# A four-layer attention and feed-forward kernel: one gate input loaded as a row and spread by a product, and a new operation order

## The chip, the cores and the metric

The kernel runs on one core of a Trainium2 chip. The number that counts is the device time of one launch in microseconds (us): 546.09 us before the change, the median of three runs (545.96 to 546.21).

A core has five instruction streams that run side by side, each strictly in its own written order: TensorE (PE, matrix products; its weight loads are listed apart as PEld), VectorE (DVE), ScalarE (ACT), GpSimd (POOL) and SyncE (SP, which here only issues DMAs). They wait for each other through semaphores. Products land in PSUM, eight banks of 128 x 512 words; everything else sits in SBUF, 128 partitions wide.

## What is computed

The input x has 2048 rows of 512. Four steps follow each other, each of the form x = x + f(layernorm(x)): attention, feed-forward, attention, feed-forward, with the same weights both times.

- Attention has 32 heads of width 16 and works in four segments of 512 rows. In a segment, scores = q kT / 4 under a causal mask, softmax, times v. Beside it runs a linear memory of the earlier segments: with phi(t) = t + 1 for t > 0 and exp(t) otherwise, a_mem = phi(q) M / (phi(q) z), where M and z gather phi(k)T v and phi(k) over the earlier segments. The head's output is g a_mem + (1 - g) a_dot, then the product with wo.
- g = sigmoid(beta), and **beta** is one vector of 32 numbers, one for each head. The kernel needs exp(beta) and exp(-beta) as 128 x 32 tiles, the same in every partition.
- Feed-forward: gelu(x w_gate) * (x w_up), then w_down, with an inner width of 1792.

## The kernel before

**Stages.** Eight passes k = 0 to 7: four segments of the first attention and feed-forward, four of the second. Within a pass come the layernorm of 4 tiles of 128 rows, their transposes, the q, k and v products, 72 score pieces in rounds, the products of probabilities with v ("flushes", line 954), wo, gate, up and down. Passes overlap: the feed-forward of pass k supplies PE with work while ACT does the exps of later scores.

**Who sets the order.** Nothing is scheduled by a compiler. The function `order` walks a clock model while it emits: it keeps a clock for each engine (`Clocks`, `Engine`), posts every operation with a ready time and a slack, and picks the next by those. `POLICY` holds some fifty numbers that steer the choice: due times of products (`qk_due`, `up_due`), slacks (`exp_slack`, `kb_slack`), how much later POOL may take over a DVE operation (`xn_pool`, `cut_pool`), how many score rounds may be ahead (`early`, `starve`). `CHANGES` can replace some of them in windows of 20 model microseconds (`Policy.move`); before the change it is empty. Once emitted, the order of each engine is fixed.

**How products are issued.** `product` (line 464) writes a 128-wide product in one of two forms. At line 476 it is one weight load and one matmul over the whole array ("whole"); at line 471 it is four weight loads and four matmuls on strips of 32 columns ("columns"), used where PE is already in that form for a flush. Scores (line 938) use a third form, strips of 16 or 32 rows ("rows"). When a bank is free but no item is ready, PE does a filler product on the tile `warm`, which is thrown away.

**The start.** This part is written by hand, not by the model:

1. SP and ACT each issue two of the four first tiles of x (line 314); ACT then issues the load of `beta_bc` to all 128 partitions (line 315); SP goes on with four halves of wk and wq, x of segment 1, wv, x of segment 2 (line 305).
2. PE does 15 products on `warm` (line 349) to be busy while the input arrives.
3. DVE takes the statistics of three tiles (line 1183), ACT of the fourth (lines 1198 and 1199). Straight after, ACT takes the two exps of beta (lines 1202 and 1203).
4. DVE writes the normalized tiles (line 544), PE transposes them (line 596), ACT copies tiles 0 and 1 out and DVE tiles 2 and 3 (lines 599 and 601), and PE does the first k and q products (lines 909 and 914), which ACT and DVE copy out (lines 1228 to 1237). DVE finishes the gate constants (lines 389 and 391), and the first scores begin.

From there on the model runs. It is told what the start took by constants: PE's clock 10.6, ACT 11.1, DVE 11.0, the DMA queue free at 13.0, x of segments 1 and 2 not before 11.85 and 14.8, v products not before 13.4.

**Other lines that come up.** 396: DVE writes the gate's column beside v. 417 and 422: masked copies of k on DVE, POOL or ACT. 461 and 462: copies out of PSUM on DVE or ACT. 514 and 522: layernorm statistics. 586: later transposes on PE. 745 and 764: phi. 1027: the addition to x. 1068, 1054 and 1151: gelu, 1151 over several tiles at once (`gelu_tiles`). 1396: the exps of the scores.

Of the kernel before, what the change touches and what calls it, by code (L numbers as in the profile page):

```python
# [11 lines left out]
ACT = mybir.ActivationFunctionType  # L12
# [3 lines left out]
BF16 = mybir.dt.bfloat16  # L16
I32 = mybir.dt.int32

P = 128
D = 512  # L20
H = 32
# [26 lines left out]
def round_of(t):  # L48
# [9 lines left out]
BANKS = 8  # L58
# [3 lines left out]
URGENT, SOON, NORMAL = -4.0, -1.5, 0.0  # L62
# [4 lines left out]


POLICY = dict(
    flush_wait=31.348, piece_slack=5.108, kb_slack=25.115, mem_slack=-15.103, margin=2.314, qk_due=0.572,  # L70
    e_q=-1.218, e_k=1.714, exp_slack=-25.107, e_slack=9.023, phi_slack=17.383, gelu_slack=6.274,
    act_evict=8.464, first_evict=0.965, gate_step=0.061, up_due=-0.553, up_step=0.062, down_due=2.078,
    down_step=0.526, upd_due=0.786, kb_act=6.552, vz_slack=-10.454, x_dve=-0.565, v0_due=-1.4, x1_at=-45.234,
    x2_at=18.289, x3_at=24.819, x3_load=-3.83, direct=4, gelu_tiles=4, look=1.769, lag=0.5, wv_at=8.591,
    xn_pool=7.037, kb_pool=5.303, cut_pool=1.107, at_pool=10.661, pe_turns=2, gate_due=0.765, shun=0.534,
    col_gap=3.33, hold=8, early=4.123, starve=0.308, near=-1.576, cap=4, soon=9.685, columns=0)

CHANGES = {
}
WINDOW = 20.0  # L80

# [204 lines left out]
def order(pol, nc, cst, seg, wrk, psp, A_x, A_wq, A_wk, A_wv, A_wo, A_beta, B_x, B_w_gate, B_w_up, B_w_down, out):  # L286

    ck = Clocks()
    ev = ck.ev
# [9 lines left out]
    wu_sb = cst.tile([P, KT, FF], BF16, name="wu_sb")  # L299
    wd_sb = cst.tile([P, FT, D], BF16, name="wd_sb")  # L300
    gel_sb = cst.tile([P, FT, L], BF16, name="gel_sb")
    beta_bc = cst.tile([P, H], BF16, name="beta_bc")

    def load(dst, src):
        nc.sync.dma_start(out=dst, in_=src)
# [6 lines left out]

    for j in range(TPS):
        (nc.scalar if j % 2 else nc.sync).dma_start(out=x_sb[:, j, :], in_=xv[:, j, :])
    nc.scalar.dma_start(out=beta_bc[:], in_=A_beta.partition_broadcast(P))
    for cols in (slice(0, D // 2), slice(D // 2, D)):
        load(w_att["k"][:, :, cols], w_view(A_wk)[:, :, cols])
        load(w_att["q"][:, :, cols], w_view(A_wq)[:, :, cols])
# [19 lines left out]
    warm = cst.tile([P, P], BF16, name="warm")  # L338
# [5 lines left out]
    ps_all = psp.tile([P, BANKS, L], F32, tag="ps", bufs=1, name="ps")  # L344
    pt_all = wrk.tile([P, PT_SLOTS, 4, UNIT], BF16, tag="pt", bufs=1, name="pt")

    def keep_warm(n, bank):
        for _ in range(n):
            nc.tensor.matmul(ps_all[:, bank, :], lhsT=warm[:], rhs=wide, start=True, stop=True)

    keep_warm(WARM, 0)

    mhalf = cst.tile([P, TPS, 1], F32, name="mhalf")
    nc.gpsimd.memset(mhalf[:], -0.5)
# [21 lines left out]
    tmp_e2 = cst.tile([P, H], F32, name="tmp_e2")  # L376
    cden = cst.tile([P, H], BF16, name="cden")
    macc = cst.tile([P, 4, P], F32, name="macc")
    tmp_e = macc[:, 0, 0:H]
# [4 lines left out]
    def by_head(va):  # L384
        return va[:, 0:TPS * VW].rearrange("p (t a h e) -> p t h a e", t=TPS, a=2, e=DH + 1)
# [8 lines left out]
    def later_constants():  # L394
        def column(va):
            nc.vector.tensor_copy(out=va[:, 0:TPS * VW].rearrange("p (t g e) -> p t g e", t=TPS, e=DH + 1)[:, :, :, DH],
                                  in_=cden[:].unsqueeze(1).to_broadcast([P, TPS, H]))
            nc.vector.memset(va[:, TPS * VW:], 0.0)

        for n, va in enumerate(vaugs[-1:] + vaugs[:-1]):  # L400
            ck.dve.post(10.5 + pol.col_gap * n, URGENT if n < 1 else NORMAL,
                        (Port(0.5), lambda va=va: column(va), lambda t, n=n: ev.update({("column", n): t})))

    def on_dve_or_pool(ready, slack, later, fast, slow, emit, told):
# [35 lines left out]
    banks = [0.0] * BANKS  # L440
# [11 lines left out]
    def evict(ps, dst, src, told, slack=NORMAL):  # L452

        taken = []

        def end(t):
            ps.read(t)
            told(t)

        first = pol.first_evict if ("scores", 0) not in ev else pol.act_evict  # L460
        ck.dve.post(ck.made(), slack, (0.673, lambda: nc.vector.tensor_copy(out=dst(), in_=src()), end), taken=taken)
        ck.act.post(ck.made(), slack + first, (0.602, lambda: nc.scalar.activation(
            out=dst(), in_=src(), func=ACT.Copy), end), taken=taken)
# [25 lines left out]
    def dense(ps, pairs):  # L489
        n = len(pairs)  # L490
        return [(Clocks.MM[512], lambda i=i, l=l, r=r: product(ps()[:], l(), r(), i == 0, i == n - 1))
                for i, (l, r) in enumerate(pairs)]
# [117 lines left out]
    class Att:  # L610
# [14 lines left out]
        def add_items(self):  # L625
            k, s = self.k, self.s
# [53 lines left out]
            def v(j):  # L680
                ps = Psum()
                pairs = [(lambda kt=kt: self.norm.xnT[:, kt, j * P:(j + 1) * P], lambda kt=kt: w_att["v"][:, kt, :])
                         for kt in range(KT)]

                def done():
                    self.counted()
                    evict(ps, lambda: by_head(self.vaug)[:, j, :, :, 0:DH],
                          lambda: ps()[:].rearrange("p (h a e) -> p h a e", a=2, e=DH), v_there)

                def v_there(t):  # L690
                    ev["v", k, j] = t
                    self.n_v += 1
                    if self.n_v == TPS:
                        ck.at(t, lambda: ck.when(lambda: not k or ("flush", k - 1, KT - 1, 1) in ev, halves))

                def halves():
                    def half(va, rows, a):
                        return va[rows, 0:TPS * VW].rearrange("p (t a v) -> p t a v", t=TPS, a=2)[:, :, a, :]

                    for a in range(2):  # L700
                        ck.sp.post(ck.pe, pol.vz_slack, (0.62, lambda a=a: nc.sync.dma_start(
                            out=half(vz, slice(C * a, C * a + C), a), in_=half(self.vaug, slice(0, C), a)), vz_sent))

                def vz_sent(t):
                    self.n_vz += 1
                    t2 = max(t + 1.4 + pol.margin, ck.dma + 1.2)
                    if self.n_vz == 2:
                        ck.at(t2 - 0.2, lambda: ev.update({("vz", k): t2}))

                return Item(lambda: k - pol.qk_due + 0.04 + 0.01 * j if k else pol.v0_due,  # L710
                            lambda: ck.has(("xnTa", k, j)) and (k or ck.pe > max(pol.wv_at, 13.4)) and
                            ck.has(("column", min(k, SETS)), by=ck.pe + 0.9) and (k <= SETS or ("flush", k - SETS, 3, 1) in ev),
                            dense(ps, pairs), done, kind="v", ps=ps, after=("xnTa", k, j))

# [3 lines left out]
            for j in range(TPS):  # L718
                items.append(v(j))
# [479 lines left out]
    nc.scalar.activation(out=spare[:, 1, :], in_=x_sb[:, TPS - 1, :], func=ACT.Square, scale=root, bias=shift[:],  # L1199
                         accum_out=n0.mv[:, TPS - 1, 1:2])  # L1200

    nc.scalar.activation(out=tmp_e, in_=beta_bc[:], func=ACT.Exp)
    nc.scalar.activation(out=tmp_e2[:], in_=beta_bc[:], func=ACT.Exp, scale=-1.0)

    first_stats(0)
    first_stats(1)
# [12 lines left out]
    a0 = att[0]  # L1219
    a0.made()  # L1220
    half = L // 2
    n0.first_turn(0)
    n0.first_turn(1)
    n0.first_turn(2)
    n0.first_turn(3)
    ps1 = ps_all[:, 1, :]
# [11 lines left out]
    gate_constants()  # L1238
    ev["xnTa", 0] = 0.0
    ev.update({("xnTa", 0, j): 0.0 for j in range(TPS)})  # L1240
    ck.pe, ck.act.free, ck.dve.free, ck.pool.free, ck.sp.free = 10.6, 11.1, 11.0, 8.1, 7.6
    banks[0:4] = [10.8, 9.45, 9.9, 10.4]
    ev["q", 0, 0] = 10.35
    a0.n_qkv = 2
    a0.k_done(0, None, 11.2)
    later_constants()
    ck.dma = 13.0
    def last_input(t):
        ck.dma_load(t, 512)
        norm_of_input(3, max(pol.x3_at, ck.dma + 1.4), 1.0)  # L1250
# [11 lines left out]
    def norm_of_input(s, at, gap):  # L1262
        for j in range(TPS):
            ck.at(at + gap * j, lambda j=j: att[s].norm.stats(j, ck.pe))

    norm_of_input(1, max(pol.x1_at, 11.85), 0.5)
    norm_of_input(2, max(pol.x2_at, 14.8), 1.0)


    streams = [(k, t) for k in range(NK) for t in range(STEPS)]  # L1270
# [42 lines left out]
    def rounds_now(idle=False):  # L1313

        if not streams or phase[0] is not None and phase[1] > pol.hold or not rounds_ready(2):
            return 0
        n, left = len(free_pairs()), len(streams)
        wait = backlog()
        if n >= 2 and (idle or left <= 4 or wait < (pol.early if streams[0][0] < 1 else pol.starve)):
            return 2  # L1320
        return 0
# [101 lines left out]
    while streams or items or opened or ck.busy():  # L1423
# [5 lines left out]
        n = rounds_now()  # L1429
# [24 lines left out]
        n = rounds_now(True)  # L1454
# [18 lines left out]
def kernel(  # L1473
# [18 lines left out]
    ctx.enter_context(tc.manual_schedule(engines=MANUAL))  # L1492
    order(Policy(POLICY, CHANGES), tc.nc, cst, seg, wrk, psp, A_x, A_wq, A_wk, A_wv, A_wo, A_beta, B_x, B_w_gate, B_w_up, B_w_down, out)

# [30 lines left out]
```

## Time and profile before

| what | value |
|---|---|
| median of three runs | 546.09 us (545.96 to 546.21) |
| device time of the profiled execution | 545.75 us |
| its span, first to last instruction | 544.0 us, so 1.75 us lie around it |
| TensorE clock granted | 0.999 of full speed over the span |
| busy | PE 531.3, PEld 276.3, DVE 443.7, ACT 434.7, POOL 305.5 us |
| chain of work that ended last | PE 88%, DVE 7%, DMA 2%, issue 2% |
| DMA | 26.95 MB, a mean of 50 GB/s |

How to read it. The busy line says how long an engine had an instruction in flight; as matmuls overlap in the pipeline, a PE that is 98% busy is one that hardly ever stood idle, and says nothing of how fast it went. The chain of waits follows the end back to the start: at each step it names what released the instruction, or the instruction before it on the same engine. In the timeline, equal neighbours are merged, and what stands in brackets is the idle time before an instruction and what ended it. The list of waits sums such idle times by who waited for whom. A few per cent of the matmul records can be missing from a trace (here 61 of 9334), and where one is, the timeline shows an apparent gap of one product that is none.

### The profile page before, as it was taken

How to read it: one execution, taken by the hardware profiler on the slowest of the kernel's cores; microseconds unless marked ns; L12 is line 12 of the kernel's file. 1: busy time of each engine (PE TensorE's matmuls, PEld its weight loads, DVE VectorE, ACT ScalarE, POOL GpSimd, SP SyncE). 2: the span in 40 equal slices, each digit the busy share in tenths (PEclk: the TensorE clock that was granted, in tenths of full speed). 3: DMA queues.
4: the chain of work that ended last, by engine and by line, in shares of the span. 5: the costliest groups of instructions: out<-in, count | busy, mean ns of one | idle time of the engine just before them, and what ended most of it. 6: DMA issues, size and time to landing. Idle time of an engine off the chain costs nothing.

```text
span 544.0 us, 21276 instructions
## 1 busy us (share of the span) xinstructions
PE 531.3 (98%) x9273; PEld 276.3 (51%) x9334; DVE 443.7 (82%) x816; ACT 434.7 (80%) x540; POOL 305.5 (56%) x359
## 2 busy tenths in 40 slices
PE   8999999999999999999999999999999999999997
PEld 4454555454545444554545555545465456555444
DVE  6998999799988999779987998889586797786342
ACT  5999989988898989989899798996879977920330
POOL 4898786369746788339993468716753265300000
PEclk9999999999999999999999999999999999999999
DMA  8406511610331123310312250221320114100001
GB/s 249 117 13 192 118 20 13 176 33 22 45 56 21 26 40 58 44 40 7 41 32 49 33 72 3 41 32 23 78 52 3 22 21 82 24 3 22 19 0 40
DMA packets 64926, 26.95 MB, mean 50 GB/s; under 512 B 49216, under 2 KB 64832, under 8 KB 64832
## 3 DMA queue, kind: packets, MB, share of 16 engines
q1 hardware_dynamic: 64400, 25.31, 22.6%
q8 instruction: 73, 1.20, 0.9%
q10 hardware_dynamic: 432, 0.27, 0.2%
q14 instruction: 21, 0.17, 0.1%
HBM read 9.71 MB, written 2.10 MB: 22 GB/s over the span
## 4 chain that ended last, share of the span: by engine, by line
PE 88%; DVE 7%; DMA 2%; issue 2%; ACT 0%; ACTq 0%; SPq 0%; DVEq 0%
PE ps L476 46%; PE ps L471 26%; PE ps L938 8%; PE ps L954 7%; DVE st L514 1%; DVE x_sb L1027 1%; DMA beta_bc<-in_A_beta_dram 1%; DVE byq L971 1%; PE ps L586 1%; DVE phiq L745 1%; PE ps L584 1%; DMA phik<-e 0%; DMA amT<-am 0%; DVE xn L544 0%; DVE e L764 0%
## 5 line engine op out<-in xcount | busy, mean ns | idle before, releaser
L1396 ACT ACTIVATE pt<-ps 128x1024 bf16<-128x1024 f32 x288 | 278.9, 1025 | 44.6 <-PE ps L938 41.1
L1343 POOL TENSOR_SCALAR_AFFINE_SELECT pt<-pt 128x256 bf16<-128x256 bf16 (+1 forms) x192 | 107.0, 571 | 118.0 <-ACT pt L1396 112.0
L1092 DVE TENSOR_TENSOR gel_sb<-gel_sb,ps 128x512 bf16<-128x512 bf16 x112 | 75.3, 682 | 33.9 <-PE ps L476 25.0
L476 PE MATMUL ps<-xnT,wu_sb 128*128 128x512 bf16 x287 | 66.8, 379 | 1.4 <-issue 1.1
L476 PE MATMUL ps<-xnT,wg_sb 128*128 128x512 bf16 x261 | 62.6, 379 | 0.9 <-issue 0.5
L764 POOL TENSOR_SCALAR e<-e 128x512 bf16<-128x512 bf16 x37 | 57.9, 1565 | 1.8 <-ACT e L741 0.7
L971 DVE STREAM_TRANSPOSE byq<-ps 128x512 f32<-128x512 f32 x64 | 45.0, 706 | 16.5 <-PE ps L954 15.9
L476 PE MATMUL ps<-wd_sb,gel_sb 128*128 128x512 bf16 (+1 forms) x293 | 56.8, 340 | 1.3 <-issue 1.0
L1348 POOL TENSOR_SCALAR_AFFINE_SELECT pt<-pt 64x1024 bf16<-64x1024 bf16 x40 | 47.8, 1196 | 15.0 <-ACT pt L1396 13.7
L1027 DVE TENSOR_TENSOR x_sb<-x_sb,ps 128x512 bf16<-128x512 bf16 (+1 forms) x68 | 42.8, 640 | 16.3 <-PE ps L476 14.7
L471 PE MATMUL ps<-wd_sb,gel_sb 128*32 128x512 bf16 (+1 forms) x792 | 47.1, 378 | 0.3 <-issue 0.3
L476 PEld LDWEIGHTS <-wu_sb 128*128 128x128 bf16 x301 | 28.2, 98 | 33.8 <-issue 0.7
L471 PE MATMUL ps<-xnT,wg_sb 128*32 128x512 bf16 x700 | 42.4, 380 | 0.0
L514 DVE BATCH_NORM_STATS2 st<-x_sb 128x6 f32<-128x512 bf16 x60 | 40.4, 674 | 0.4 <-DMA x_sb<-in_A_x_dram 0.3
L476 PEld LDWEIGHTS <-wg_sb 128*128 128x128 bf16 x273 | 25.3, 98 | 28.8 <-issue 0.2
L476 PEld LDWEIGHTS <-gel_sb 128*128 128x128 bf16 x306 | 28.3, 98 | 22.7 <-issue 1.1
L954 PE MATMUL ps<-pt,vaug 128*32 128x256 bf16 (+2 forms) x1344 | 34.6, 238 | 0.0
L417 POOL TENSOR_SCALAR kx<-kf,masks 128x512 bf16<-128x512 bf16 x20 | 33.5, 1678 | 1.2
L471 PE MATMUL ps<-xnT,wu_sb 128*32 128x512 bf16 x588 | 34.1, 379 | 0.0
L1151 ACT ACTIVATE gel_sb<-gel_sb 128x2048 bf16<-128x2048 bf16 (+1 forms) x21 | 33.2, 1643 | 0.0
L544 DVE TENSOR_SCALAR xn<-x_sb,mv,rs 128x512 bf16<-128x512 bf16 x58 | 31.3, 592 | 2.2 <-POOL rs L532 1.9
L954 PEld LDWEIGHTS <-vaug 128*32 128x32 bf16 x1344 | 27.8, 97 | 10.4 <-issue 2.2
(147 smaller groups left out, 883.6 us busy)
## 6 DMA issues: line engine op xcount, KB each, us to landing
vz<-vaug SPq DMA_DIRECT2D x14, 136.0 KB, 2.9
wg_sb<-in_B_w_gate_dram SPq DMA_DIRECT2D x8, 224.0 KB, 4.6
wu_sb<-in_B_w_up_dram SPq DMA_DIRECT2D x8, 224.0 KB, 4.3
wd_sb<-in_B_w_down_dram SPq DMA_DIRECT2D x7, 256.0 KB, 4.2
x_sb<-in_A_x_dram SPq DMA_DIRECT2D x3, 512.0 KB, 7.3
out_dram<-x_sb SPq DMA_DIRECT2D x12, 128.0 KB, 1.8
xnT<-xn SPq DMA_TRANSPOSE x40, 2.5
wk_sb<-in_A_wk_dram SPq DMA_DIRECT2D x2, 256.0 KB, 6.0
```

Source lines behind the costliest of these rows:

```text
L471: nc.tensor.matmul(out[r], lhsT=lhsT[:, r], rhs=rhs, start=start, stop=stop, tile_position=(0, 32 * c))
L476: nc.tensor.matmul(out, lhsT=lhsT, rhs=rhs, start=start, stop=stop)
L514: nc.vector.bn_stats(out=self.st6[:, 0, :], in_=x_sb[:, self.tt0 + j, :])
L764: lambda eng: eng.tensor_scalar(out=e[0][:], in0=e[0][:], scalar1=1.0, scalar2=None, op0=ALU.min), summed)
L938: nc.tensor.matmul(ps_all[:, bank, o + c0:o + c0 + n], lhsT=lhsT, rhs=self.q[rows, b, q0:q0 + n], start=True, stop=True, tile_position=(32 ...
L954: nc.tensor.matmul(ps()[32 * j:32 * j + 32, q0:q0 + n], lhsT=va[:, ki * VW + g:ki * VW + g + 32], rhs=pt_all[:, places[i], j, c0:c0 + n], ...
L971: nc.vector.transpose(out=self.byq[:, par, :, :].rearrange("p a c -> p (a c)"), in_=ps()[:])
L1027: ck.dve.post(ck.made(), slack, (0.15 + 0.00104 * (c1 - c0), lambda: nc.vector.tensor_tensor(out=xt, in0=xt, in1=ps()[:, 0:c1 - c0], op=AL ...
L1092: ck.dve.post(ck.made(), NORMAL, (0.683, lambda: nc.vector.tensor_tensor(out=g, in0=g, in1=ps()[:], op=ALU.mult), lambda t: (ps.read(t), e ...
L1343: nc.gpsimd.affine_select(out=view, in_=view, pattern=[[0, 4], [0, n], [1, C]], compare_op=ALU.is_ge, fill=0.0, base=C, channel_multiplier=-1)
L1348: nc.gpsimd.affine_select(out=view, in_=view, pattern=[[0, 4 * TPS], [1, C]], compare_op=ALU.is_ge, fill=0.0, base=0, channel_multiplier=-1)
L1396: nc.scalar.activation(out=pt_all[:, s0:s0 + 2, 2 * p:2 * p + 2, :].rearrange("p r h c -> p h r c"), in_=ps_all[:, pair[0]:pair[1] + 1, :] ...
```

## The change

**Beta.** The load by ACT's queue brings one row of 32 numbers to one partition (`beta_row`). After the 15 products on `warm`, PE multiplies a row of ones by that row, which gives beta in every partition of one PSUM bank. The two exps read that bank, and stand on ACT behind the copies of the first two transposed tiles instead of ahead of them.

**What the model is told of the start.** Its clocks start about 0.5 us earlier (SP's 1.1), and inputs are taken to be there 1.5 to 1.9 us earlier.

**The policy.** Nearly all numbers of `POLICY` are new, and 24 of the 20-us windows have values of their own in `CHANGES`. The largest steps: the gelu over stored tiles goes over 2 at a time instead of 4, x of the last segment is loaded earlier (`x3_load`), v may start earlier (`wv_at`). Two names that no line reads come and go (`columns`, `x_whole`).

The diff, cut:

```diff
 POLICY = dict(
-    flush_wait=31.348, piece_slack=5.108, kb_slack=25.115, mem_slack=-15.103, margin=2.314, qk_due=0.572,
...
-    x2_at=18.289, x3_at=24.819, x3_load=-3.83, direct=4, gelu_tiles=4, look=1.769, lag=0.5, wv_at=8.591,
+    flush_wait=25.841, piece_slack=8.493, kb_slack=22.44, mem_slack=-19.299, margin=2.0, qk_due=0.589,
...
+    x3_at=25.984, x3_load=-21.059, direct=4, gelu_tiles=2, look=4.778, lag=0.5, wv_at=-4.63, xn_pool=3.908,
...
 CHANGES = {
+    0: dict(kb_slack=20.795, margin=2.743, qk_due=0.557, exp_slack=-28.04, phi_slack=16.773, up_due=-0.201,
...
+    25: dict(gate_step=0.076, upd_due=0.833, gate_due=0.58),
 }
-    beta_bc = cst.tile([P, H], BF16, name="beta_bc")
+    beta_row = cst.tile([1, H], BF16, name="beta_row")
-    nc.scalar.dma_start(out=beta_bc[:], in_=A_beta.partition_broadcast(P))
+    nc.scalar.dma_start(out=beta_row[:], in_=A_beta.partition_broadcast(1))
     keep_warm(WARM, 0)
+    beta_ps = ps_all[:, BANKS - 1, 0:H]
+    nc.tensor.matmul(beta_ps, lhsT=warm[0:1, :], rhs=beta_row[:], start=True, stop=True)
-            ck.dve.post(10.5 + pol.col_gap * n, URGENT if n < 1 else NORMAL,
+            ck.dve.post(10.0 + pol.col_gap * n, URGENT if n < 1 else NORMAL,
-                            lambda: ck.has(("xnTa", k, j)) and (k or ck.pe > max(pol.wv_at, 13.4)) and
+                            lambda: ck.has(("xnTa", k, j)) and (k or ck.pe > max(pol.wv_at, 11.5)) and
-    nc.scalar.activation(out=tmp_e, in_=beta_bc[:], func=ACT.Exp)
-    nc.scalar.activation(out=tmp_e2[:], in_=beta_bc[:], func=ACT.Exp, scale=-1.0)
     n0.first_turn(0)
     n0.first_turn(1)
+    nc.scalar.activation(out=tmp_e, in_=beta_ps, func=ACT.Exp)
+    nc.scalar.activation(out=tmp_e2[:], in_=beta_ps, func=ACT.Exp, scale=-1.0)
     n0.first_turn(2)
-    ck.pe, ck.act.free, ck.dve.free, ck.pool.free, ck.sp.free = 10.6, 11.1, 11.0, 8.1, 7.6
-    banks[0:4] = [10.8, 9.45, 9.9, 10.4]
-    ev["q", 0, 0] = 10.35
+    ck.pe, ck.act.free, ck.dve.free, ck.pool.free, ck.sp.free = 10.1, 10.6, 10.5, 8.1, 6.5
+    banks[0:4] = [10.3, 8.95, 9.4, 9.9]
+    ev["q", 0, 0] = 9.85
-    a0.k_done(0, None, 11.2)
+    a0.k_done(0, None, 10.7)
-    ck.dma = 13.0
+    ck.dma = 11.5
-    norm_of_input(1, max(pol.x1_at, 11.85), 0.5)
-    norm_of_input(2, max(pol.x2_at, 14.8), 1.0)
+    norm_of_input(1, max(pol.x1_at, 10.0), 0.5)
+    norm_of_input(2, max(pol.x2_at, 12.9), 1.0)
```

What it does to the built order, counted from the two programs:

| PE, DVE, ACT, POOL | before | after |
|---|---|---|
| 512-wide products of lines 471 and 476, whole | 1149 | 1013 |
| the same in column strips | 674 | 810 |
| of these, fillers on `warm` | 31 | 31 |
| changes between whole, rows and columns | 301 | 297 |
| PE instructions in all | 18670 | 19356 |
| gelu over 4 stored tiles / over 2 | 14 / 7 | 0 / 35 |
| masked copies of k, instructions on DVE / POOL / ACT | 10 / 26 / 28 | 14 / 28 / 22 |
| causal mask rounds on DVE / half rounds on POOL | 12 / 40 | 10 / 44 |
| cut of phi on DVE / POOL | 11 / 37 | 14 / 34 |

Narrower products are equally many in both and move between the forms as well; scores and flushes are the same. Between the first score and the first v product PE has 10 products of 512 columns and one further group of scores before, and 6 products and one further group after.

## The prediction

> **What bounds the kernel now.** I read the page's head first, then the chain of waits, then PE's own waits, then the start in the timeline.
>
> ```profile
> PE 531.3 (98%) x9273; PEld 276.3 (51%) x9334; DVE 443.7 (82%) x816; ACT 434.7 (80%) x540; POOL 305.5 (56%) x359
> ...
> PE 88%; DVE 7%; DMA 2%; issue 2%; ACT 0%; ACTq 0%; SPq 0%; DVEq 0%
> ```
>
> PE is busy nearly always and makes up 88% of the chain. So a saving must come from one of four places: PE does less, each product goes faster, PE waits less, or PE starts earlier. The list of who PE waits for shows how little waiting is left:
>
> ```profile
> PE ps L476 <- issue: 4.3, 27, 0.2
> PE ps L349 <- DVE warm L340: 1.1, 1, 1.1
> PE ps L596 <- DVE xn L544: 1.0, 2, 0.7
> ```
>
> The 4.3 us of "issue" are 27 gaps of 0.16, each where the record of one product is missing; they are no waits. As the listed idle time undercounts a pipelined engine, I also took the starts of all PE products, gave each pair of neighbours the median interval of its kind, and added up: from the first score (10.56 us) to the last product (540.60) that makes 524.8 us of the 530.0 that passed. **Waits behind the start hold 5.2 us**; about 2.3 of them sit at a dozen places of 0.06 to 0.5 us (the main ones at 32.7, 71.7, 79.4, 112 to 113, 126 to 128, 136.4, 397.4 and 400.0), the rest is spread thinly.
>
> The chain of the first 12 us shows what the change aims at:
>
> ```profile
> 1.71 5.38 DMA beta_bc<-in_A_beta_dram
> 7.09 0.02 issue
> 7.11 0.23 ACT macc L1202
> 7.34 0.12 ACT tmp_e L1203
> 7.46 0.98 ACT xnT L599 x2
> 8.44 0.04 issue
> 8.48 0.60 PE ps L909 x4
> ```
>
> The load of beta, landing at 7.09, is on the path: ACT stands in front of it, and the copies of the transposed tiles, which PE needs, queue behind the exps.
>
> **Part 1, the start.** Without beta ahead of it, ACT takes copy 0 when its transposes are through. The timeline has them here:
>
> ```profile
> 6.63 0.72 PE L596 MATMUL ps<-ident,xn 128*128 128x128 bf16 x8 [0.73 <-DVE xn L544]
> ...
> 7.63 0.72 PE L596 MATMUL ps<-ident,xn 128*128 128x128 bf16 x8 [0.29 <-DVE xn L544]
> ```
>
> The eight of tiles 0 and 1 end at 7.35, with tile 0's four about 0.35 earlier, at 7.0. Copy 0 then takes 0.53 (half of 1.06), copy 1 follows at about 7.46 and ends at 8.0 instead of 8.44, a gain of 0.44. But PE is in its own way: the transposes of tiles 2 and 3 wait for DVE and POOL, which the change leaves alone, and their last start is 8.13. So the first k product can start at 8.19 instead of 8.48. **Gain 0.29 us**, with bounds 0 (something else holds ACT) and 0.44 (all of the two exps, 230 and 213 ns). From there to the first score the chain is products and copies without slack, so 0.29 arrives there, at 10.27. The exps themselves move to about 8.05, between copy 1 and the copy at line 1228, which was at 9.12 and can start at 8.83; 0.44 fits, so they cost nothing. If copy 1 were 0.35 later they would be on the path again.
>
> The new product on PE costs at most one 128-column interval, 0.056 us, and stands in the 0.73 us in which PE waits for DVE: nothing. It does add a wait. All transposes stand behind it in PE's queue, so if the row lands after 6.63 the start slips. In the trace ACT's last x tile lands at 4.30 and the first beta packets of 64 bytes run at 3.9; one row is one such packet, so I take a landing near 4.5, with the old 7.09 as the other bound.
>
> The load of the other inputs may gain as well:
>
> ```profile
> 4.00:6.50 2.50, 1.90 (x9) 0.69 (x7) 2.32 (x10) 1.54 (x4) 0.88 (x2) 1.00 0.67 170
> 6.50:8.00 1.50, 1.09 (x13) 0.72 (x14) 1.19 (x5) 0.89 (x4) 0.63 (x1) 1.00 1.15 327
> ```
>
> The last column is GB/s. While the 128 beta packets run (3.9 to 6.7), the DMA engines move 170 GB/s, and right after them 327. If the packets are the cause, 2.5 x 157 / 327 = 1.2 us come back, and x of segment 1 (11.30), wv (12.72) and x of segment 2 (14.22) land at 10.1 to 13.0. The Trainium skill, page "DMA: Bandwidth & Descriptors", section "Queues, rings and completion order", says each DMA engine takes turns between its queues, a packet at a time, by which ACT's small transfers would indeed delay SP's. Whether they come earlier hardly matters for the sum. With the old landings DVE would wait 0.3 us longer at 11.33, and the first v product, set at 10.27 + 2.5 = 12.8, still meets its weights.
>
> **Part 2, PE's work.** The two orders hold the same products: 1823 of 512 columns, 31 of them fillers, in both. 136 move from the whole array to four column strips. Late in the trace stand long runs of each:
>
> ```profile
> 474.18 22.45 PE ps L471 x416
> ...
> 517.15 10.95 PE ps L476 x50
> ```
>
> 416 strips are 104 products, 216 ns each; the whole form gives 10.95 / 51 = 215 (one record is missing). The move costs nothing. The Trainium skill, page "TensorEngine Tiling (Array Packing)", section "Restrictions", says column tiling turns off fast weight loading, which speaks against 136 more such products. The trace has 97 ns for a strip's load and 98 ns for a whole one, so by the trace it costs nothing here.
>
> Changes of form fall from 301 to 297. One costs about 0.096 us (a whole product is followed by a score after 312 ns instead of 216). With the same medians laid on the new order, the stretch from first score to last product is 524.4 instead of 524.8. **Gain 0.37 us.**
>
> **Part 3, the other engines.** With the durations of before: ACT gets 35 gelus of 1075 ns for 14 of 1927 and 7 of 1075 (+3.1), loses six masked copies (-3.8) and gains copies out of PSUM (+1.3): +0.6. DVE +0.3, POOL +2.2 (four half mask rounds of 1196, two more masked copies net, fewer cuts). SP issues the same DMAs. None of these bounds the kernel, so nothing is added.
>
> **Part 4, the waits.** This is the term that no row prices. Six of these places lie in 20 to 40, 60 to 80 and 100 to 140 us, where DVE is busy 18.8 to 19.6 of 20 us and PE waits on its chain:
>
> ```profile
> 67.44 0.60 DVE x_sb L1027
> 68.04 1.06 DVE e L745 x2
> 69.11 0.35 DVE st L514
> 69.46 2.45 DMA phik<-e
> 71.91 0.05 issue
> 71.95 0.60 PE ps L476 x7
> ```
>
> Here an addition to x stands on DVE between the steps of phi. In the new order it comes behind the fourth phi(k); DVE has 1.7 us less work ahead of that point, and 3.3 us less ahead of the sixteenth addition to x. The fillers in front (21 before, 22 after) are fixed in the order, so only the wait beyond them can go. These places hold 1.6 us; I take **half, 0.8 us**. Bounds: 2.6 (all named waits go and a tenth of the spread ones), and on the other side the full lengthening of gelu, 3.1, as a loss.
>
> **Sum.** 0.29 + 0.37 + 0.8 = 1.5 us off the profiled execution's 545.75: 544.3. The median of the runs is 0.34 above that execution, so **544.6 us**.
>
> **Rivals.** A measurement of this kernel can tell about 0.2% (1.1 us) from no change, so faster means below 545.0, slower above 547.2.
>
> - *The waits only move* (C): parts 1 and 2 alone, 546.09 - 0.66 = 545.4. For it: PE's fixed order meets four other engines at new places, and thinly spread waits come back. Against: DVE's lighter load ahead of the two late chains.
> - *All named waits go, and a tenth of the rest* (B): 546.09 - 0.66 - 2.6 = 542.9. For it: PE has the lead over ACT (ACT waits 41 us for scores), so small shifts on DVE suffice. Against: no order so full is free of waits.
> - *ACT becomes the bound in the gelu phases* (slower): each gelu over 4 tiles becomes two, and while they run no exp can, as the table is another. That is 3.1 us over 7 phases. It decides where ACT has no idle left: it is busy 19.2 of 20 us at 80 to 100 and 19.7 at 340 to 360. Against: most of ACT's idle time ends on a score from PE. In full: 546.09 - 0.66 + 3.1 = 548.5; with half the phases hit, 547.0.
> - *The row lands as late as before*: transposes at 7.1 instead of 6.63, so 0.46 lost instead of 0.29 won: 545.4.
> - *Strips pay for their loads*, the page's rule above: 136 x 97 ns exposed is 13 us, 558. Against: 216 ns in both forms.
>
> **Chances.** Forecast 40%, B 20%, C 20%, the late row 3%, ACT as the bound 16%, dearer strips 1%. Faster 0.60, same 0.23, slower 0.17. The range runs from B with the start at its better bound (542.7) to half of the gelu price (547.0).
>
> **What would show it.** Right: no beta DMA in the chain of the first 12 us, line 909 at 8.2, the first score at 10.3, x of segment 1 landing nearer 10 than 11.3, and the wait at 71.7 smaller. Wrong: PE's transposes waiting for a DMA, idle PE ended by an ACT exp or gelu around the gelu phases, intervals above 216 ns in strips, or more than 5.2 us between the priced work and the elapsed time behind the first score.

## The result, and the profile after

The changed kernel takes **547.73 us** (median of 7 runs, 547.29 to 548.08), the kernel before 545.98 beside it (7 runs, 545.75 to 546.21): a ratio of 1.0031, 95% interval 1.0020 to 1.0042. It is slower by 1.75 us, where 1.5 less was forecast.

The profiled execution took 548.06 us with a span of 545.87. The busy line and the first line of the chain of waits, in the changed kernel's page:

```profile
PE 538.4 (99%) x9677; PEld 278.5 (51%) x9677; DVE 443.5 (81%) x821; ACT 434.9 (80%) x550; POOL 311.3 (57%) x360
...
PE 13%; DVE 0%; issue 0%
```

PE looks busier than before (538.4 for 531.3) in a longer span, which shows how little the busy line says here: where a record is missing it counts a gap, and this trace misses none. The chain is of no use this time. It covers 13% of the span and then finds no releaser, so the time is taken apart by the starts of the PE products, as in the prediction:

| part, in us | before | after | difference |
|---|---|---|---|
| up to the first score | 10.56 | 10.95 | +0.39 |
| PE's work from there to the last product, at the medians of before | 524.79 | 524.42 | -0.37 |
| waits of PE in that stretch | 5.26 | 7.12 | **+1.86** |
| last product to the end of the span | 3.39 | 3.39 | 0 |
| outside the span | 1.76 | 2.19 | **+0.43** |

The rows add up to 2.31 and not to 1.75, as the profiled execution of after lies 0.33 above its median and that of before 0.23 below its own. How much counts as work and how much as waiting depends on what is taken as one kind of pair: when the place within a group of strips is told apart as well, the same starts give 526.24 and 526.10 us of work, and 3.80 and 5.42 of waits. Either way the waits grow, by 1.6 to 1.9.

So there are three places to look at: the start, the waits, and time in which no instruction is recorded at all. Of the waits, 1.3 of the 1.86 lie in 60 to 80 us (1.88 for 0.59), and 0.6 in 120 to 140 (1.38 for 0.75). The list of whom PE waits for has two new ones in those stretches, the first two lines here (the third belongs to the start):

```profile
PE ps L534 <- DVE x_sb L1085: 0.9, 1, 0.9
PE ps L534 <- DVE byq L1029: 0.5, 1, 0.5
PE ps L967 <- ACT xnT L657: 0.5, 1, 0.5
PE ps L534 <- ACT pt L1454: 0.4, 1, 0.4
```

Line numbers of the body are 58 higher than before: 534 is the whole-array product of 476, 1085 the addition to x of 1027, 1029 and 803 are 971 and 745. The timeline around the two new waits, PE, DVE and POOL together:

```profile
71.95 2.35 POOL L1406 TENSOR_SCALAR_AFFINE_SELECT pt<-pt 64x1024 bf16<-64x1024 bf16 x2 [1.19 <-ACT pt L1454]
...
73.26 1.07 DVE L948 COPY zacc<-zk 128x4 f32<-128x4 f32 x1
...
77.11 0.38 PE L534 MATMUL ps<-warm 128*128 128x512 bf16 x1 [0.54 <-DVE byq L1029]
...
121.65 1.16 POOL L1047 TENSOR_TENSOR aT<-aT,amT 128x512 bf16<-128x512 bf16 x1
121.72 1.64 DVE L803 SCALAR_TENSOR_TENSOR phiq<-q,e 128x512 bf16<-128x512 bf16 x1
...
129.00 0.65 DVE L1085 TENSOR_TENSOR x_sb<-x_sb,ps 128x512 bf16<-128x512 bf16 x1
...
129.70 1.67 PE L534 MATMUL ps<-wo_sb,aT 128*128 128x512 bf16 x7 [0.90 <-DVE x_sb L1085]
```

Read the second column, the duration. A copy of four words per partition takes 1.07 us, and it ends with POOL's half mask (71.95 + 2.35 = 74.30). The addition of phi(q) takes 1.64 us for its usual 0.69, and it starts 0.07 after an addition of POOL's that ends at 122.81: 122.8 + 0.6 is about where it ends (123.36). DVE loses 0.9 us each time, and a few instructions later PE waits for a bank that DVE should have emptied, the second time by the addition to x that ends at 129.65. The same instructions before:

```profile
74.02 0.14 DVE L890 COPY zacc<-zk 128x4 f32<-128x4 f32 x1
...
120.14 1.16 POOL L989 TENSOR_TENSOR aT<-aT,amT 128x512 bf16<-128x512 bf16 x1
120.21 1.63 DVE L745 SCALAR_TENSOR_TENSOR phiq<-q,e 128x512 bf16<-128x512 bf16 x1
...
127.38 1.25 DVE L1027 TENSOR_TENSOR x_sb<-x_sb,ps 128x512 bf16<-128x512 bf16 x2
```

The copy met no running POOL instruction there. The addition did, just as long, but PE has other products to do behind it: up to 129 us the timeline shows no wait of PE's for DVE.

The kernel's own clock model, which set the order, says the same from another side. Against the trace of before it is right within 0.5 us all the way (medians over 10 us); against the trace of after it falls behind by 0.75 at the start, by another 0.7 at 76 to 80 us and by 1.0 at 128 to 132. It takes neither stop into account: the copy has the plain cost 0.154 (line 948), not the kind (`Port`, line 139) that waits for POOL, and POOL's addition is marked `soft` (line 1050), for which DVE is charged 0.15.

### The profile page after: what moved, and what is told of

It reads as the page before. It is cut to its first block, busy times and chain, and to the rows that moved or that the text cites. A ratio compares the mean times of both kernels' runs of the same rounds, so it can differ in the third digit from the quotient of the medians.

```text
span 545.9 us, 22040 instructions
## 1 busy us (share of the span) xinstructions
PE 538.4 (99%) x9677; PEld 278.5 (51%) x9677; DVE 443.5 (81%) x821; ACT 434.9 (80%) x550; POOL 311.3 (57%) x360
## 5 line engine op out<-in xcount | busy, mean ns | idle before, releaser
L1406 POOL TENSOR_SCALAR_AFFINE_SELECT pt<-pt 64x1024 bf16<-64x1024 bf16 x44 | 52.5, 1193 | 12.5 <-ACT pt L1454 9.2
L534 PE MATMUL ps<-xnT,wu_sb 128*128 128x512 bf16 x251 | 57.7, 380 | 0.0
L529 PE MATMUL ps<-wd_sb,gel_sb 128*32 128x512 bf16 (+1 forms) x1032 | 57.6, 368 | 0.0
L1029 DVE STREAM_TRANSPOSE byq<-ps 128x512 f32<-128x512 f32 x64 | 45.0, 705 | 10.4 <-PE ps L1012 8.7
L534 PE MATMUL ps<-wd_sb,gel_sb 128*128 128x512 bf16 (+1 forms) x246 | 47.8, 343 | 0.0
L529 PE MATMUL ps<-xnT,wu_sb 128*32 128x512 bf16 x788 | 45.0, 379 | 0.0
L475 POOL TENSOR_SCALAR kx<-kf,masks 128x512 bf16<-128x512 bf16 x24 | 41.6, 1735 | 1.2
L534 PEld LDWEIGHTS <-wu_sb 128*128 128x128 bf16 x251 | 23.6, 98 | 28.3 <-issue 0.7
L529 PEld LDWEIGHTS <-gel_sb 128*32 128x32 bf16 x1032 | 25.7, 97 | 21.4 <-issue 1.5
L519 DVE CAST gel_sb<-ps 128x512 bf16<-128x512 f32 x42 | 28.2, 682 | 8.3 <-PE ps L529 4.3
L1209 ACT ACTIVATE gel_sb<-gel_sb 128x1024 bf16<-128x1024 bf16 x35 | 34.9, 1068 | 0.0
L1012 PEld LDWEIGHTS <-vaug 128*32 128x32 bf16 x1344 | 27.9, 97 | 10.3 <-issue 2.0
```

What stands on the lines that cost most here:

```text
L475: return lambda: eng.tensor_scalar(out=kx[:, :, C * which:C * which + P], in0=kf, scalar1=masks[:, which:which + 1], scalar2=None, op0=ALU ...
L529: nc.tensor.matmul(out[r], lhsT=lhsT[:, r], rhs=rhs, start=start, stop=stop, tile_position=(0, 32 * c))
L534: nc.tensor.matmul(out, lhsT=lhsT, rhs=rhs, start=start, stop=stop)
L1012: nc.tensor.matmul(ps()[32 * j:32 * j + 32, q0:q0 + n], lhsT=va[:, ki * VW + g:ki * VW + g + 32], rhs=pt_all[:, places[i], j, c0:c0 + n], ...
L1029: nc.vector.transpose(out=self.byq[:, par, :, :].rearrange("p a c -> p (a c)"), in_=ps()[:])
L1406: nc.gpsimd.affine_select(out=view, in_=view, pattern=[[0, 4 * TPS], [1, C]], compare_op=ALU.is_ge, fill=0.0, base=0, channel_multiplier=-1)
```

## The experiments

"Before" in the tables below is the kernel before on the same chip: 546.11, 546.10 and 545.90 us for the three groups. Intervals are 95%.

### Which half of the change costs?

Theory O: the new order costs the time, the beta row does not. Theory S: the start does. Theory C concerns the clock: the 15 products on `warm` are done at half rate (0.427 us apart for 0.216) until TensorE's clock rises, and in the profile of after that lasted to 6.6 us. This is its start:

```profile
1.11 6.15 PE L405 MATMUL ps<-warm 128*128 128x512 bf16 x15 [1.11 <-DVE warm L396]
7.19 0.18 PE L409 MATMUL ps<-beta_row,warm 1*128 1x32 bf16 x1
7.30 1.07 PE L654 MATMUL ps<-ident,xn 128*128 128x128 bf16 x16
8.87 0.60 PE L967 MATMUL ps<-xnT,wk_sb 128*128 128x256 bf16 x4 [0.50 <-ACT xnT L657]
...
10.95 0.40 PE L996 MATMUL ps<-wd_sb 16*128 16x256 bf16 x12 [0.17 <-DVE tmp_e L449]
```

The 15 products took 6.15 us (4.79 before), so the transposes stood in PE's queue until 7.30 though their data was there for 6.63.

**e1_beta_only**: the kernel before with the edits for beta alone (row, product, place of the exps), policy and clocks as before.

```diff
-    nc.scalar.dma_start(out=beta_bc[:], in_=A_beta.partition_broadcast(P))
+    nc.scalar.dma_start(out=beta_row[:], in_=A_beta.partition_broadcast(1))
...
     keep_warm(WARM, 0)
...
+    nc.tensor.matmul(beta_ps, lhsT=warm[0:1, :], rhs=beta_row[:], start=True, stop=True)
...
```

> The kernel before with the beta edits alone: one row loaded, the product, the two exps behind the copies of tiles 0 and 1. The order of every engine is otherwise that of before. Theory O (the new order loses the time, in waits of PE near 63 to 82 and at 128 us): this kernel is 0.3 us faster than before when the clock rises early, up to 0.4 slower when the 15 products on warm all run at half clock as they did in the profile after; so between -0.3 and +0.4. Theory S (the start loses it: a late PE at the start carries through to the end and disturbs what follows): +1 us or more.

**e2_order_only**: the other half, the new `POLICY`, `CHANGES` and the clocks' constants, with beta loaded as before.

> The changed kernel with the old load of beta to all partitions and the exps at their old place; order otherwise as after. Theory O: 1.4 to 2.2 us slower than before, with the waits at 71, 76 and 128 us there again. Theory S: within 0.5 us of before.

**e3_after_warm11** and **e4_beta_warm11**: the changed kernel and e1 with `WARM = 11` for 15.

> The changed kernel with 11 products on warm instead of 15. Theory C (the clock's rise comes by chance of phase, early or late; late, the 15 products end at 7.2 and hold up the transposes): the transposes start when DVE has the first tile (6.5), whatever the clock, and the first score comes at 10.3 to 10.4; 0.3 to 0.7 us faster than the changed kernel in a late start, the same in an early one. Rival (the warm products are what brings the clock up; with fewer it rises later): transposes and first k and q products at half clock, first score at 11 or later, so 0.3 us or more slower than the changed kernel.

> The kernel before with the beta edits and 11 products on warm. Theories O and C together: 0.2 to 0.7 us faster than before and no slower than the beta edits alone with 15. Theory S, or a clock that needs the 15 products: slower than before.

| kernel | us | ratio to before | first score | waits behind it |
|---|---|---|---|---|
| e1_beta_only | 545.73 | 0.9999 (0.9990 to 1.0007) | 10.25 | 5.85 |
| e2_order_only | 548.81 | 1.0049 (1.0037 to 1.0061) | 10.43 | 8.41 |
| e3_after_warm11 | 548.23 | 1.0039 (1.0027 to 1.0051) | 11.98 | 7.23 |
| e4_beta_warm11 | 545.75 | 0.9994 (0.9985 to 1.0002) | 11.84 | 5.22 |

Theory O holds and S falls: the order alone costs 2.7 us, the row alone nothing that can be measured. The 2.7 is more than the 1.4 to 2.2 expected, and the halves do not add up to the 1.75 of the whole change: with the new order the row seems to be worth about 1 us, and why was not tried. In e1 the start came out within 0.02 us as worked out:

```profile
8.17 0.60 PE L911 MATMUL ps<-xnT,wk_sb 128*128 128x256 bf16 x4
...
10.25 0.40 PE L940 MATMUL ps<-wd_sb 16*128 16x256 bf16 x12 [0.17 <-DVE tmp_e L393]
```

But its span of 544.28 is no shorter than before's. The 0.31 us are given back in waits (+0.59), the largest 0.55 at 112.8 and 0.82 at 397, at places where before waited too. The second is no wait for another engine. It lies inside one product, between its first and its second strip, and no instruction there waits for a semaphore. Here it is in e1, then in before:

```profile
398.35 1.91 PE L473 MATMUL ps<-wd_sb,gel_sb 128*32 128x512 bf16 x32 [0.60 <-issue]
```

```profile
398.07 1.26 PE L471 MATMUL ps<-wd_sb,gel_sb 128*32 128x512 bf16 x20 [0.31 <-issue]
```

In e8, e10 and e11, which have the same PE order, it is 0.33, 0.52 and 0.71, so it varies from execution to execution; what causes it is not shown.

Fewer products on `warm` are no remedy. The start of e3:

```profile
6.79 0.72 PE L654 MATMUL ps<-ident,xn 128*128 128x128 bf16 x8 [1.41 <-DVE xn L602]
7.80 1.03 PE L654 MATMUL ps<-ident,xn 128*128 128x128 bf16 x8 [0.28 <-DVE xn L602]
8.62 1.06 PE L967 MATMUL ps<-xnT,wk_sb 128*128 128x256 bf16 x4
9.48 1.90 PE L972 MATMUL ps<-xnT,wq_sb 128*128 128x256 bf16 x8
```

PE stands idle for 1.41 us, and from 7.85 on the products are 0.213 apart for 0.109: the clock has fallen back, until 11.2. In e4 it fell at 7.75 and rose again at 11.1. This is what the rival of e3 forecast (first score at 11 us or later), not theory C, which had it at 10.3 to 10.4. In both the profiled execution is about 1 us above the median, so probably not every launch fares like that. At the median, 11 products take the same as 15 with the old order (545.75 and 545.73), and 0.5 us more with the new one (548.23 and 547.73, which is within the spread of the launches).

### Are the two collisions the loss?

Theory P: the two DVE instructions that wait for POOL cause the new waits, and without them the order costs nothing. Rival: the waits are spread and come back elsewhere. **e5_after_again** is the changed kernel once more.

> The changed kernel once more, beside the next three. Theory C (the clock rises at a moment of its own): the 15 products on warm take another time than 6.15 us, and the first score moves with them, between 10.25 and 10.95. The rival (the change makes the clock rise late): 6.1 to 6.2 us again. The waits behind the first score should again hold about 7.1 us, with 0.9 at 75 to 76 us and 1.05 at 128 us.

The 15 products took 5.86 us this time, and the first score came at 10.67: the clock rises at another moment in the same kernel, as theory C has it. The two waits are there again (0.88 and 1.05).

**e6_zacc_reduce** moves the four words with a sum over one element in place of the copy, **e8_before_zacc** does the same to the kernel before, as a control:

```diff
-  steps = [(0.154, lambda: nc.vector.tensor_copy(out=zacc[:], in_=self.zk[:]), kept),
+  steps = [(0.154, lambda: nc.vector.reduce_sum(out=zacc[:], in_=self.zk[:].unsqueeze(2), axis=mybir.AxisListType.X), kept),
```

> The changed kernel with the 4-word copy of zacc done as a sum over one element, which gives the same numbers in another form of instruction. Theory P (a copy on DVE that finds a GpSimd operation running waits until that ends; here it waits 0.92 us for half a mask, and PE then waits 0.88 at 75 to 76 us): the instruction takes 0.2 us instead of 1.07, the waits at 75 to 76 us fall under 0.3, and the time falls by 0.6 to 0.9 us. Rivals: every form of DVE instruction waits there (no change), or PE at 76 us waits for something else that comes as late (DVE faster, time unchanged).

> The kernel before with zacc as a sum, as a control. Its copy took 0.14 us and met nothing on GpSimd. Theory P: no change, within 0.2 us. If the form of the instruction itself is worth something: faster here too.

**e7_zacc_phiq** is e6 with that one phi(q) addition put behind the two statistics instructions that follow it on DVE:

```diff
...
+    def emit_one(self, emit):
+        n, self.n_emitted = self.n_emitted, self.n_emitted + 1
+        if n == self.hold_at:
+            self.held = emit
+            return
+        emit()
+        if n == self.hold_to:
+            self.held()
...
+        self.dve.hold_at, self.dve.hold_to = 187, 189
```

> The kernel with zacc as a sum, and one phi(q) addition on DVE (the one at 121.72 us, 1.63 us long) moved behind the statistics that follow it, so that it no longer meets the GpSimd addition to aT. Theory P: that addition takes 0.7 us, DVE is 0.9 us earlier at 123 us, the wait of 1.05 us at 128 us falls under 0.3, and the time falls by another 0.7 to 1.0 us, to within 0.4 us of the kernel before. Rival: the bank at 128 us is late for another reason; no change beside the kernel with zacc alone.

| kernel | us | ratio to before | waits in 60 to 80 | in 120 to 140 | in all |
|---|---|---|---|---|---|
| e5_after_again | 547.68 | 1.0032 (1.0020 to 1.0044) | 1.49 | 1.38 | 7.36 |
| e6_zacc_reduce | 547.07 | 1.0021 (1.0012 to 1.0029) | 1.95 | 1.38 | 7.19 |
| e7_zacc_phiq | 545.83 | 0.9996 (0.9987 to 1.0004) | 0.95 | 0.18 | 5.42 |
| e8_before_zacc | 546.25 | 1.0003 (0.9994 to 1.0011) | 0.86 | 0.62 | 5.70 |

The collision goes in e6, POOL's half masks standing where they stood:

```profile
72.02 2.35 POOL L1406 TENSOR_SCALAR_AFFINE_SELECT pt<-pt 64x1024 bf16<-64x1024 bf16 x2 [1.19 <-ACT pt L1454]
...
73.33 0.12 DVE L948 TENSOR_REDUCE zacc<-zk 128x4 f32<-128x4 f32 x1
```

And in e7 the second, with PE going on without the wait (13 products in one stretch, where the changed kernel has 2 and 7 with 0.90 of idleness between):

```profile
121.86 0.69 DVE L814 SCALAR_TENSOR_TENSOR phiq<-q,e 128x512 bf16<-128x512 bf16 x1
...
127.27 2.98 PE L545 MATMUL ps<-wo_sb,aT 128*128 128x512 bf16 x13
```

Theory P holds. The copy cost 547.68 - 547.07 = 0.6 us, the addition 547.07 - 545.83 = 1.2. The first step alone is not clear of the noise, as the intervals of e5 and e6 overlap; the second is, and so are both together (1.85). The 1.2 is more than the wait of 1.05: behind the moved addition two more DVE instructions came out shorter, 0.69 us for 0.91 (line 1037) and 0.41 for 0.90 (line 1047), as they meet POOL elsewhere. In e6 the waits at 75 to 76 us fell from 0.88 to 0.17; the 1.95 of the table holds a wait of 1.0 at 62.9, ahead of the edit, where the other profiles of the new order have 0 to 0.4. The waits of 0.70 and 1.05 behind the two collisions, in contrast, stand within 0.01 in every profile of the new order that has no edit against them. The control moves by nothing that can be measured: it is not the instruction that costs, but where it meets POOL.

### What costs 0.44 us outside the span?

Every run has a device time and a span, and the difference stays within 0.08 of a kernel's mean (spans are listed to 0.1). The mean is 1.72 in the kernel before, e1, e4 and e8, but 2.16 in the changed kernel, e2, e3, e5, e6 and e7, which all have the new order. Behind the changed kernel's last instruction (545.87), the DMA view of 546 to 549 us has one packet:

```profile
DMA packets 1, 0.01 MB, mean 3 GB/s; under 512 B 0, under 2 KB 0, under 8 KB 0
## 3 DMA queue, kind: packets, MB, share of 16 engines
q14 instruction: 1, 0.01, 0.6%
```

It is a block of code, 8192 bytes. Other blocks of this queue come as DVE, ACT or POOL reaches every 128th or so of its instructions. The last of POOL's came at 463 us in the trace of before, at POOL's 446th record of 464. In the new order POOL has 452 (fewer waits; 360 instructions that do work, for 359), and it comes to its 446th only in the closing lines of the program, at 545.2 us. Theory F: this late block costs the 0.44. Rival: PE's longer program (19356 for 18670 instructions) or something else in the order does.

All four kernels add memsets of one small tile to POOL behind its last work, where it is idle:

```diff
+    for _ in range(16):
+        nc.gpsimd.memset(mhalf[:], -0.5)
     return ck.pe + 0.0005 * ck.count
```

**e9_e7_pool16**: 16 of them in e7, 468 instructions in all.

> The kernel with the copy as a reduction and the held addition (545.83), plus 16 memsets on POOL behind its last work. In every run so far the device time exceeds the span by 1.72 us where the old order runs and by 2.16 where the new one does, and the traces of the new order show one 8 KB packet of code on the second instruction queue about 1.2 us behind the last instruction; the old order has none there, its packet being fetched at 463 us when POOL is at its 446th instruction. With the new order POOL comes to that instruction only in the closing lines (452 in all against 464). Theory F (the late code block costs the 0.44): POOL now passes the place at about 500 us, no code packet behind the end, 1.72 us outside the span, 545.4 us in all. Rival (PE's longer program, 19356 for 18670 instructions, or the order in some other way): 2.16 stays, 545.8.

**e10_before_pool116** and **e11_before_pool100**: 116 and 100 of them in the kernel before.

> The kernel before with 116 memsets on POOL behind its last work, 580 instructions for 464: a block of 128 more than the 452 of the changed kernel, so that POOL should come to its next block of code in the closing lines. Theory F: one code packet behind the last instruction, 2.16 us outside the span in place of 1.72, 546.5 in all, with the span as it was. Rival (PE's program): 1.72, 546.1.

> The control: 100 memsets, 564 instructions, 16 fewer than in the run beside it, so that POOL ends short of its next block. Theory F: no code packet behind the end, 1.72 us outside the span, 546.1. If more instructions on POOL cost something by themselves, both runs show it alike.

**e12_after_pool16**: 16 of them in the changed kernel.

> The changed kernel with nothing but 16 memsets on POOL behind its last work. Theory F: 1.72 us outside the span in place of 2.16, 547.3 for 547.7; the two collisions of DVE with POOL stay, so it stays slower than before. Rival: 547.7.

| kernel | POOL's records | code behind the end | outside the span | us | ratio to before |
|---|---|---|---|---|---|
| e9_e7_pool16 | 468 | no | 1.73 | **545.29** | 0.9989 (0.9981 to 0.9998) |
| e10_before_pool116 | 580 | yes | 2.17 | 546.54 | 1.0011 (1.0002 to 1.0020) |
| e11_before_pool100 | 564 | no | 1.73 | 546.15 | 1.0002 (0.9994 to 1.0011) |
| e12_after_pool16 | 468 | no | 1.72 | 547.10 | 1.0023 (1.0014 to 1.0031) |

Theory F holds on all four, in both directions: sixteen instructions more take the 0.44 away, and 116 more bring it to the kernel before, while 100 do not. PE's longer program is still there in e9 and e12, so the rival falls. Over all 14 profiles the packet stands behind the end in the seven kernels with 2.16, and in none of the seven with 1.72. One detail did not come out. In e9 the block was expected at about 500 us, at POOL's 446th record; it came at 459.9, at the 437th, which the changed kernel passes at about 462 without a packet. So what decides the moment of the fetch is not shown, nor why the end waits for it. The same view of e12 for 546 to 549 us is empty, and e10 has its packet in 544.8 to 549:

```profile
DMA packets 0, 0.00 MB, mean 0 GB/s; under 512 B 0, under 2 KB 0, under 8 KB 0
```

```profile
q14 instruction: 1, 0.01, 0.8%
```

e9 is also the fastest kernel of the study. Its profile has the start that the prediction worked out, and 5.05 us of waits behind the first score:

```profile
6.62 0.72 PE L665 MATMUL ps<-ident,xn 128*128 128x128 bf16 x8 [0.62 <-DVE xn L613]
...
8.19 0.60 PE L978 MATMUL ps<-xnT,wk_sb 128*128 128x256 bf16 x4
...
10.27 0.40 PE L1007 MATMUL ps<-wd_sb 16*128 16x256 bf16 x12 [0.17 <-DVE tmp_e L460]
```

## Why the prediction was wrong, point by point

**The account.** The change costs 1.75 us. Taken away one after the other, the copy gives back 0.6, the addition 1.2 and the code block 0.44, together 2.3; what is left, e9, stands 0.6 below the kernel before (0.1 to 1.0 by its interval). Parts 1 and 2 of the sum came to 0.66, but that the two agree is luck as far as these runs show: part 1 gave nothing on average, as the next paragraph says, and e1, with part 1 alone, is no faster. Where e9's 0.6 comes from stays open. The smaller waits of the new order (0.42 at 71 us, some 0.7 from 314 to 334) were not tried.

**Part 1, the start: the path was right, but the gain comes only when the clock rises early.** First k product at 8.17 to 8.19 and first score at 10.25 to 10.27 in e1 and e9 (forecast 8.19 and 10.27). The row's packet ran at 3.6 us in the changed kernel (3.8 in e1). There the inputs came 1.2 us earlier, as worked out from the 170 GB/s: x of segment 1 at 10.06 (11.30), wv at 11.57 (12.72), x of segment 2 at 13.06 (14.22). Overlooked was the clock. With beta off the path, the 15 products on `warm` are next on it, and they end when the clock happens to rise; the trace of before, with 4.79 us for them, was the second shortest of twelve such profiles (4.76 to 6.33). In after (6.15) they push the transposes to 7.30 and the first score to 10.95. In the seven profiles with the row and 15 products the first score comes at 10.25 to 11.12 us, 10.63 on average; in the five without the row at 10.43 to 10.92, 10.63 on average too. So the 0.29 was read off one start with an early clock. The prediction asked what is late next of ACT and DVE, and not of the products in PE's queue.

**Part 2, PE's work: the premise was right, the size is not tested.** The 524.42 of the table had to agree with the forecast, as it is the same sum, medians of before on the new order; with the finer kinds of pairs the gain is 0.14 for 0.37. What the trace of after does show is that four strips and a whole product still start 216 ns apart, so the rival of strips that pay for their loads is dead.

**Part 3, the other engines: nothing, as forecast.** ACT 434.9 (434.7 before), DVE 443.5 (443.7); POOL's 311.3 (305.5) is 5.8 more where 2.2 were worked out, and none of them bounds the kernel by its sum. What the step left out is that an engine's number of instructions can decide whether a block of code arrives behind the end.

**Part 4, the waits: this step failed.** It took half of 1.6 us of waits as won, because DVE has 1.7 and 3.3 us less work ahead of the late chains. The waits grew by 1.86 instead. DVE's work ahead of a point is not its delay there: an instruction of DVE's can stand for the rest of a POOL instruction, 0.9 us in one go, and that is half of the 1.7 it was said to be relieved of. Counted at the medians of before, DVE has 1.15 us less work from 12 us on ahead of the addition to x that PE waits for at 129.65 (the seventh), and yet starts it at 129.00 for 127.38. The 3.3 less, ahead of the sixteenth addition, stands at 192 us, behind the places up to 140 for which it was used. The collisions were in the trace of before to be seen: 34 instructions of DVE more than 0.3 us over the median of their form, together 17.4 us (29 and 14.5 after). The new order has fewer of them, and two at places where PE waits a few instructions later. The bound "below nothing" was worked out from gelus, on the wrong engine.

**The bounds and the rivals.** The slower rival had the right side and the wrong cause: no wait of PE ends on a gelu, and that its 547.0 to 548.5 hold the time is chance. "The waits only move" (545.4) comes nearest to what the order does without its two collisions and the code block (545.29).

**The base: a term put at nothing.** The sum took what lies around the span, 1.75, as fixed. It was 2.19.

## What to carry to other kernels

Where PE follows a fixed order and four engines feed it, do not weigh the work of an engine ahead of a wait: look in the new order for its two-input additions and its copies within SBUF, see which POOL instruction runs when each of them starts, and ask what is queued behind. When a move costs 1 us only because of where it meets another engine, change the instruction's form or its place by two, before searching for another order. And compare device time minus span for each kernel: a constant step in it is a matter of the program's ends, and here 16 idle instructions were worth 0.44 us.

## What the runs showed of the hardware that was not expected

- **DVE waits for POOL to the end of its instruction, in some pairs of forms.** The copy of 128x4 f32 took 1.07 for 0.14, phi(q)'s addition 1.64 for 0.69; the sum over one element took 0.12 in the same place, beside the same running half mask, and the statistics beside them 0.68 as ever. The Trainium skill, page "SBUF — State Buffer", section "SBUF: two separate sides", has the rule that the prediction should have weighed: the port pair that the two share is locked for a whole instruction, against a DVE instruction in a mode that uses both ports, or with two SBUF inputs where POOL's instruction reads SBUF too; a f32 copy within SBUF is named as one of the first sort. The traces agree with it in both cases, but not everywhere. In the 14 profiles phi(q)'s addition started 147 times with more than 0.5 us of a POOL instruction left. It took over 0.3 us longer in all 28 starts beside a mask, all 11 beside an addition to aT and 37 of 51 beside a cut of phi, and in none of the 57 beside masked copies of k, a layernorm's normalization or its small `rs` product.
- **A late code block costs 0.44 us at the end.** Blocks of 8192 bytes come in at some 20 other moments of a run; no run here looks at what those cost. The Trainium skill, page "Runtime: NRT & Kernel Launch", section "Instruction fetch mechanics", calls the fetch of the next block mostly hidden; at the end of this kernel it is not. It gives blocks of 16 KiB, and the traces have 16384 bytes for PE and 8192 for the others.
- **The clock's rise comes at a moment of its own.** With the same products from 1.1 us on, they went from 0.427 apart to 0.216 at 4.0, 5.2, 5.3, 5.7, 6.2, 6.5, 6.6 and 7.0 us in eight of the twelve profiles with 15 products; by the granted clock all twelve lie between 3.9 and 7.05. In e3 the changes lie 3.4 us apart (4.45, 7.85, 11.2), and the fall came after 1.41 us of idleness with gaps behind it.
